# The second half of wq issued from ScalarE's DMA queue, beside the first half on the sync queue, both with 32 KiB rows

## The chip, the cores and the metric

The kernel runs on one core of a Trainium2 chip. The metric is the device time of one execution in microseconds (us); several executions are taken of each kernel, in turns with the kernel it is compared with on the same chip. The profile is one execution more, taken by the hardware profiler; its span is 1.8 us shorter than the device time of the same execution (136.8 against 138.62 for the kernel before).

The engines are PE (TensorE, matmuls; PEld is its weight load), DVE (VectorE), ACT (ScalarE), POOL (GpSimd) and SP (SyncE, which here issues loads only). A name with q (SPq, ACTq) is the engine's instruction sequencer issuing a DMA.

## The reference

One decode step of a transformer layer for a batch of 4, one token each. All tensors are bfloat16.

```python
# B, D = 4, 1024; Hq, Hkv, Dh = 32, 4, 128; Sk = 8192; F = 3584
W = min(4096, max(256, Sk // 4))                       # 2048: the last W keys
q = (layernorm(x) @ wq).reshape(B, 1, Hq, Dh)          # wq 1024 x 4096
scores = einsum(q, k_cache[:, :, Sk-W:]) * Dh ** -0.5  # 8 query heads share one kv head
o = einsum(softmax(scores), v_cache[:, :, Sk-W:])
h = x + o @ wo                                         # wo 4096 x 1024
n = layernorm(h)
out = h + (silu(n @ w1) * (n @ w3)) @ w2               # w1, w3 1024 x 3584; w2 3584 x 1024
```

With four tokens, each weight and each cache entry is used by very few products. The kernel must read wq (8.4 MB), the last 2048 keys and values (8.4 MB each), wo (8.4 MB), w1 and w3 (7.3 MB each) and w2 (7.3 MB): 55.6 MB.

## The kernel before

All large loads go through one pool of five SBUF slots of 32 KiB per partition (4 MiB in all 128 partitions), in one fixed order, on the sync queue. Five slots are filled at the start; each further load is called for when a slot's last reader has been written into the program.

```python
stream = ctx.enter_context(tc.tile_pool(name="stream", bufs=5))
SLOT = 16384; RQ = 4                                   # RQ: chunks of 128 rows of wq in one slot
wq_v = A_wq.rearrange("(p i) n -> p (i n)", i=KC)      # 8 chunks, 8 KiB each per partition

def load_rows(src, n, r0, pieces):
    t = stream.tile([P, SLOT], BF16, tag="s")
    i = 0
    for m in pieces:                                   # one DMA for each piece of m chunks
        nc.sync.dma_start(
            out=t[:, i * n : (i + m) * n], in_=src[:, (r0 + i) * n : (r0 + i + m) * n]
        )
        i += m
    return [t[:, k * n : (k + 1) * n] for k in range(i)]

plan = (
    [("wq", load_rows, (wq_v, N_Q, c, [2, 2] if c == 0 else [4])) for c in range(0, KC, RQ)]
    + [("k", load_kv, (A_k_cache, b)) for b in range(0, B, BS)]
    + ...                                              # v, wo, w1, w3, w2
)
# x_sb <- A_x and later four small loads of x go through nc.scalar
load_next(5)                                           # wq, wq, k, k, v
...
for kc in range(KC):                                   # q = layernorm(x) @ wq : 64 matmuls
    wq_t = loaded["wq"][kc]
    ...
            nc.tensor.matmul(q_ps[...], lhsT=xnT[:, kc, :], rhs=wq_t[:, c0 : c0 + 512],
                             start=(kc == 0), stop=(kc == KC - 1))
    if kc % RQ == RQ - 1:
        load_next()
q_sb = act.tile([P, CQ], BF16)                         # q, scaled, then transposed into qz
...
for u, (b, n) in enumerate(units):                     # K stage: 16 units
    ...                                                # 16 transposes of K on PE into PSUM,
                                                       # copied out by DVE and ACT in turn: kT
    if u >= 1:
        emit_scores(u - 1)                             # 4 matmuls of qz with kT
```

After the K stage come softmax, the product with V (OT_ps), wo (y_ps), the second LayerNorm (hnT), w1 (g_ps), w3 (u_ps), w2 (y_ps again) and the output. The order in which each engine finally runs its instructions is decided when the kernel is built, by a scheduler: it need not be the order of the source.

Of the kernel before, what the change touches and what calls it, by code (L numbers as in the profile page):

```python
# [19 lines left out]
def kernel(  # L20
# [13 lines left out]
    nc = tc.nc  # L34
# [7 lines left out]
    KC = D // P  # L42
# [38 lines left out]
    RQ = 4  # L81
    RO = 16
    BS = 2
    wq_v = A_wq.rearrange("(p i) n -> p (i n)", i=KC)
# [2 lines left out]
    w3_v = B_w3.rearrange("(p i) n -> p (i n)", i=KC)  # L87
    w2_v = B_w2.rearrange("(p i) n -> p (i n)", i=IF)

    def load_rows(src, n, r0, pieces):  # L90

        t = stream.tile([P, SLOT], BF16, tag="s")
        i = 0
        for m in pieces:
            nc.sync.dma_start(  # L95
                out=t[:, i * n : (i + m) * n], in_=src[:, (r0 + i) * n : (r0 + i + m) * n]
            )
            i += m
        return [t[:, k * n : (k + 1) * n] for k in range(i)]

    def load_kv(src, b):
# [11 lines left out]

    N_Q, N_F = Hq * Dh, F
    plan = (
        [("wq", load_rows, (wq_v, N_Q, c, [2, 2] if c == 0 else [4])) for c in range(0, KC, RQ)]
        + [("k", load_kv, (A_k_cache, b)) for b in range(0, B, BS)]
        + [("v", load_kv, (A_v_cache, b)) for b in range(0, B, BS)]
        + [("wo", load_rows, (wo_v, D, c, [RO])) for c in range(0, IO, RO)]
        + [("w1", load_rows, (w1_v, N_F, c, [RQ])) for c in range(0, KC, RQ)]  # L120
        + [("w3", load_rows, (w3_v, N_F, c, [RQ])) for c in range(0, KC, RQ)]
        + [("w2", load_rows, (w2_v, D, 0, [16])), ("w2", load_rows, (w2_v, D, 16, [5, 4, 2, 1]))]
# [349 lines left out]
```

## Time and profile before

| | before |
|---|---|
| time, median of 3 runs | 138.68 us (138.57 to 138.72) |
| span of the profile | 136.8 us |
| bytes read | 55.59 MB |
| q matmuls begin (16, 16 and 32 of them) | 8.2, 12.9, 22.6 us |
| last K scores (start of the softmax maximum) | 57.2 us |
| first gate matmuls (w1) | 94.1 us |
| first matmul on the last piece of w2 | 133.1 us |

First, parts 2 and 3 of the page of the kernel before. DMA is the busy share of the 16 DMA engines in tenths, in 40 equal slices (3.4 us each); GB/s is what they moved; q1 is the sync queue, q10 ScalarE's, q8 the fetches of instructions (packets, MB, share of 16 engines).

```profile
DMA  5999999999999999999999999999999999998950
GB/s 156 437 413 512 393 402 436 421 436 436 417 431 421 436 431 431 431 438 474 460 393 412 426 426 449 427 441 411 436 436 441 427 419 433 441 460 361 420 220 5
...
q1 hardware_dynamic: 3168, 55.58, 95.2%
q8 instruction: 8, 0.13, 0.3%
q10 hardware_dynamic: 60, 0.02, 0.1%
```

The DMA engines are full from the second slice to nearly the last. Almost everything is on the sync queue. Part 4, the chain of waits that ended last, by engine and by line:

```profile
DMA 42%; PE 31%; ACT 12%; DVE 8%; issue 3%; SPq 1%; ACTq 0%; DVEq 0%
DMA t<-in_B_w_dram 26%; DMA t<-in_A_wq_dram 15%; PE kt_ps L261 10%; ACT kT L267 5%; PE scores_ps L246 5%; PE OT_ps L324 5%; PE y_ps L351 5%; ACT z L302 3%; PE q_ps L213 3%; DVE rmax L278 2%; ACT Pm L283 2%; SPq L95 1%; DVE pT L292 1%; PE g_ps L400 1%; DVE z L298 1%
```

Read alone, this chain says that PE and ACT share the blame: 43% of the span. The timeline says how to take it. Its columns are start, duration, engine, line, operation, number, and in brackets how long the engine was idle before and what ended the idleness. L213 are the q matmuls (the second and third stretch wait for wq; the first starts at 8.18 behind a mask that DVE finishes), L278 the first instruction after the last K scores, L400 and L430 the gate, up and last down matmuls; the SPq line is the issue of w1's second half:

```profile
8.18 1.88 PE L213 MATMUL q_ps<-t,xnT 128*4 128x512 bf16 x16 [1.20 <-DVE same L203]
...
12.91 1.87 PE L213 MATMUL q_ps<-t,xnT 128*4 128x512 bf16 x16 [2.86 <-DMA t<-in_A_wq_dram]
...
22.61 3.58 PE L213 MATMUL q_ps<-t,xnT 128*4 128x512 bf16 x32 [7.83 <-DMA t<-in_A_wq_dram]
...
57.21 2.29 DVE L278 TENSOR_REDUCE rmax<-scores_ps 128x1 f32<-128x2048 f32 x1 [1.48 <-PE scores_ps L246]
...
75.71 0.33 SPq L95 DMA_DIRECT2D t<-in_B_w_dram  x1
...
94.12 1.70 PE L400 MATMUL g_ps<-t,hnT 128*32 128x448 bf16 x32 [2.27 <-DVE hnT L388]
99.21 3.17 PE L400 MATMUL g_ps<-t,hnT 128*32 128x448 bf16 x32 [3.39 <-DMA t<-in_B_w_dram]
...
107.66 3.17 PE L400 MATMUL u_ps<-t,hnT 128*32 128x448 bf16 x32 [5.28 <-DMA t<-in_B_w_dram]
...
116.11 3.18 PE L400 MATMUL u_ps<-t,hnT 128*32 128x448 bf16 x32 [5.28 <-DMA t<-in_B_w_dram]
...
133.14 0.41 PE L430 MATMUL y_ps<-t,hgT 128*32 128x256 bf16 x4 [0.24 <-DMA t<-in_B_w_dram]
```

Each stage near the end begins when its load lands. The stages in the middle do not wait for loads, but the loads do not wait for them either: the sync queue issues far ahead. The nearest call is w1's second half, issued at 75.7 us when the first V slot comes free; wo's second half and w1's first half are then still queued or under way.

### The profile page before, as it was taken

To read this page: it belongs to the slowest core of one execution; us is meant where nothing else is said; L and a number is where in the kernel's file an instruction comes from. 1 tells how busy PE (TensorE), PEld (TensorE's weight loads), DVE (VectorE), ACT (ScalarE), POOL (GpSimd) and SP (SyncE) were. 2 spreads that over 40 slices of the span, in tenths; PEclk is the share of its full clock that TensorE was granted. 3 is DMA by queue.
4 is the path that set the end of the run, shared out by engine and by line. 5 is a ranking of instruction groups with operands and counts; after the bars stand their busy time and mean duration, and the time that the engine had idled before them with its cause. 6 is when DMAs were issued, how large, how long until landed. Compare 5 with 4: busy or idle time off the path is not lost.

```text
span 136.8 us, 2307 instructions
## 1 busy us (share of the span) xinstructions
PE 70.0 (51%) x1035; PEld 43.7 (32%) x1035; DVE 42.5 (31%) x73; ACT 31.1 (23%) x36; POOL 1.7 (1%) x8
## 2 busy tenths in 40 slices
PE   0152303799898989503275646954090530802940
PEld 0110001296565656200065644732030210301820
DVE  6440000224343434445962003053003980160000
ACT  0400000126473737354765000000005000000001
POOL 5000000000000000000000000000000000000000
PEclk9999999999999999995555555599959555595595
DMA  5999999999999999999999999999999999998950
GB/s 156 437 413 512 393 402 436 421 436 436 417 431 421 436 431 431 431 438 474 460 393 412 426 426 449 427 441 411 436 436 441 427 419 433 441 460 361 420 220 5
DMA packets 3238, 55.75 MB, mean 407 GB/s; under 512 B 376, under 2 KB 408, under 8 KB 668
## 3 DMA queue, kind: packets, MB, share of 16 engines
q1 hardware_dynamic: 3168, 55.58, 95.2%
q8 instruction: 8, 0.13, 0.3%
q10 hardware_dynamic: 60, 0.02, 0.1%
q14 instruction: 2, 0.02, 0.0%
HBM read 55.59 MB, written 0.01 MB: 406 GB/s over the span
## 4 chain that ended last, share of the span: by engine, by line
DMA 42%; PE 31%; ACT 12%; DVE 8%; issue 3%; SPq 1%; ACTq 0%; DVEq 0%
DMA t<-in_B_w_dram 26%; DMA t<-in_A_wq_dram 15%; PE kt_ps L261 10%; ACT kT L267 5%; PE scores_ps L246 5%; PE OT_ps L324 5%; PE y_ps L351 5%; ACT z L302 3%; PE q_ps L213 3%; DVE rmax L278 2%; ACT Pm L283 2%; SPq L95 1%; DVE pT L292 1%; PE g_ps L400 1%; DVE z L298 1%
## 5 line engine op out<-in xcount | busy, mean ns | idle before, releaser
L267 ACT COPY kT<-kt_ps 128x1024 bf16<-128x1024 bf16 x16 | 15.9, 1013 | 13.0 <-PE kt_ps L261 13.0
L261 PE MATMUL kt_ps<-ident,t 128*128 128x128 bf16 x256 | 17.7, 229 | 0.0
L261 PEld LDWEIGHTS <-t 128*128 128x128 bf16 x256 | 15.7, 103 | 4.9 <-issue 4.9
L265 DVE COPY kT<-kt_ps 128x1024 bf16<-128x1024 bf16 x16 | 11.1, 692 | 16.1 <-PE kt_ps L261 16.1
L213 PE MATMUL q_ps<-t,xnT 128*4 128x512 bf16 x64 | 7.3, 623 | 11.9 <-DMA t<-in_A_wq_dram 10.7
L400 PEld LDWEIGHTS <-hnT 128*32 128x32 bf16 x128 | 4.8, 128 | 21.9 <-issue 19.0
L400 PE MATMUL u_ps<-t,hnT 128*32 128x448 bf16 x64 | 6.4, 575 | 10.6 <-DMA t<-in_B_w_dram 10.6
L324 PE MATMUL OT_ps<-z,t 128*128 128x32 bf16 x256 | 7.5, 188 | 7.6 <-ACT z L302 5.0
L246 PE MATMUL scores_ps<-kT,qz 128*32 128x512 bf16 x64 | 9.9, 609 | 2.9 <-ACT kT L267 2.9
L430 PE MATMUL y_ps<-t,hgT 128*32 128x256 bf16 x112 | 5.8, 374 | 8.4 <-DMA t<-in_B_w_dram 8.4
L324 PEld LDWEIGHTS <-t 128*128 128x128 bf16 x256 | 7.4, 105 | 8.3 <-issue 8.3
L400 PE MATMUL g_ps<-t,hnT 128*32 128x448 bf16 x64 | 4.9, 464 | 5.7 <-DMA t<-in_B_w_dram 3.4
L430 PEld LDWEIGHTS <-hgT 128*32 128x32 bf16 x112 | 4.4, 131 | 10.4 <-issue 6.0
L213 PEld LDWEIGHTS <-xnT 128*4 128x4 bf16 x64 | 2.0, 111 | 16.3 <-issue 16.0
L440 ACT CAST res<-y_ps 128x256 bf16<-128x256 f32 x1 | 0.4, 373 | 28.9 <-PE y_ps L430 28.9
L351 PE MATMUL y_ps<-t,o 128*32 128x256 bf16 x128 | 6.1, 382 | 0.8 <-DVE o L340 0.8
L223 DVE TENSOR_SCALAR q_sb<-q_ps 128x512 bf16<-128x512 f32 x1 | 0.7, 692 | 17.7 <-PE q_ps L213 17.7
L302 ACT ACTIVATE z<-pt_ps,mask 128x512 bf16<-128x512 f32 x8 | 5.3, 687 | 3.5 <-DVE z L298 3.5
L294 PE MATMUL pt_ps<-pT,perm 128*128 128x512 bf16 x4 | 2.4, 607 | 6.8 <-DVE pT L292 6.8
L298 DVE TENSOR_SCALAR z<-pt_ps,mask 128x512 bf16<-128x512 f32 x8 | 5.5, 740 | 1.2 <-ACT z L302 0.8
L414 DVE RECIPROCAL eg<-eg 128x896 f32<-128x896 f32 x1 | 5.8, 5752 | 0.0
L351 PEld LDWEIGHTS <-o 128*32 128x32 bf16 x128 | 4.6, 136 | 3.1 <-DVE o L340 1.9
(73 smaller groups left out, 41.0 us busy)
## 6 DMA issues: line engine op xcount, KB each, us to landing
t<-in_B_w_dram SPq DMA_DIRECT2D x4, 3584.0 KB
t<-in_A_k_cache_dram SPq DMA_DIRECT2D x4, 2048.0 KB, 25.5
t<-in_A_v_cache_dram SPq DMA_DIRECT2D x4, 2048.0 KB, 41.6
t<-in_A_wo_dram SPq DMA_DIRECT2D x2, 4096.0 KB, 40.9
t<-in_A_wq_dram SPq DMA_DIRECT2D x2, 2048.0 KB, 9.6
t<-in_A_wq_dram SPq DMA_DIRECT2D x1, 4096.0 KB, 20.9
t<-in_B_w_dram SPq DMA_DIRECT2D x1, 4096.0 KB, 35.9
t<-in_B_w_dram SPq DMA_DIRECT2D x1, 1280.0 KB, 32.9
```

The costliest lines, as they stand in the source:

```text
L213: nc.tensor.matmul(q_ps[QD * g : QD * g + B, hf * 512 : (hf + 1) * 512], lhsT=xnT[:, kc, :], rhs=wq_t[:, c0 : c0 + 512], start=(kc == 0), ...
L246: nc.tensor.matmul(scores_ps[QD * g : QD * (g + 1), n * 512 : (n + 1) * 512], lhsT=qz[:, b, g * QD : (g + 1) * QD], rhs=kT_v[:, g, :, :], ...
L261: nc.tensor.transpose(out=kt_ps[:, jj, :], in_=k_v[:, n * NJ + t * TB + jj, :], identity=ident[:])
L265: nc.vector.tensor_copy(out=kT[:, t * TB : (t + 1) * TB, :], in_=kt_ps[:])
L267: nc.scalar.copy(out=kT[:, t * TB : (t + 1) * TB, :], in_=kt_ps[:])
L298: nc.vector.tensor_scalar(out=z[:, :, g, :], in0=pt_ps[:], scalar1=mask[:, g : g + 1], scalar2=None, op0=ALU.mult)
L302: nc.scalar.mul(out=z[:, :, g, :], in_=pt_ps[:], mul=mask[:, g : g + 1])
L324: nc.tensor.matmul(OT_ps[:, b, :], lhsT=loaded["v"][b][:, j, :], rhs=PTz[j // NJ][:, (j % NJ) * B + b, :, :], start=(j == 0), stop=(j == J ...
L351: nc.tensor.matmul(y_ps[QD * j : QD * (j + 1), :], lhsT=o4[:, i, :, :].rearrange("p b s -> p (b s)"), rhs=loaded["wo"][i][:, j * CG : (j + ...
L400: nc.tensor.matmul(out_ps[QD * j : QD * (j + 1), hf, :HF], lhsT=hnT[:, k, :], rhs=loaded[kind][k][:, c0 : c0 + HF], start=(k == 0), stop=( ...
L414: nc.vector.reciprocal(out=eg[:], in_=eg[:])
L430: nc.tensor.matmul(y2_ps[QD * j : QD * (j + 1), :], lhsT=hgT[:, i, :], rhs=loaded["w2"][i][:, j * CG : (j + 1) * CG], start=False, stop=(i ...
```

## The change

The intent is that the two halves of wq, the first large thing that PE waits for, are issued from two queues and come in side by side, and that both move in rows of 32 KiB per partition, the first half in one load instead of two.

```diff
-    def load_rows(src, n, r0, pieces):
+    def load_rows(src, n, r0, pieces, eng=nc.sync):
...
-            nc.sync.dma_start(
+            eng.dma_start(
...
-        [("wq", load_rows, (wq_v, N_Q, c, [2, 2] if c == 0 else [4])) for c in range(0, KC, RQ)]
+        [("wq", load_rows, (wq_v, N_Q, c, [4], nc.sync if c == 0 else nc.scalar)) for c in range(0, KC, RQ)]
```

## The prediction

> **What bounds it now: DMA bytes.** In the 40-slice view the DMA row reads 9 from the second slice to nearly the last, at 400 to 460 GB/s. In the trace's DMA packets the weights run back to back, 1.7 to 132.8 us: 55.6 MB in 131 us. After the last landing only 4 us remain. The chain of waits says the same of the end (a w load issued at 97.2, landing at 133.1), but fills its middle, 22.6 to 94 us, with PE and ACT work: those stages run close behind the DMA without holding it up. The sync queue always has work: its loads take 35 to 43 us from issue to landing. The tightest refill is w1's second half, issued at 75.7 when v's first slot comes free, while about 12 us of loads are queued (estimate from the landings).
>
> **What the change does.**
> - Moves an issue (0.42 us) from the sync queue to ScalarE's, ahead of the small x loads and LayerNorm there: about 0.4 us later. No cost: q waits for wq far longer.
> - 16 KiB rows for the first half of wq become 32 KiB. A 16 KiB packet takes 611 ns, a 32 KiB one 1213 ns: over 16 engines 16 x 0.611 = 9.78 against 8 x 1.213 = 9.70, gain 0.07 us.
> - Two rings at once. The Trainium skill, "DMA: Bandwidth & Descriptors", section "Issuing engines are not separate DMA queues", says that loads from both queues run on the same 16 engines and interleave, saving only issue time. The trace before cannot show it (ScalarE's queue carries 0.02 MB), but one ring already moves 433 GB/s with all engines busy: a second has nothing to add.
> - The order of landing changes. Before, wq landed in pieces at 8.1, 12.9 and 22.6 us, and half the q matmuls (2 x 1.88 us) ran under the load. If the rings share evenly, both halves land near 22 to 23, and all matmuls (2 x 3.6 us) come after: q done near 29 instead of 26.2.
> - The built order of PE puts 19 K transposes among and before the q transposes, which hides their 0.7 us wait. K stage ends near 59.4 instead of 57.2 (estimate).
>
> **Critical path.** That 2 us delay runs through softmax, PV and wo, to the first gate matmuls near 96 instead of 94.1. The second gate half waits for w1's landing at 99.2, where PE now idles 3.4 us; the wait shrinks to about 1.3. At 107.7 another 5.3 us of idle follow. So the delay is swallowed, and buffer releases 2 us later eat into a 12 us queue without emptying it. Net -0.07 us, with a small loss possible from interleaving.
>
> **Predicted time: 138.7 us, range 138.1 to 139.5.** Chances: faster by over 2% 0.02, within 2% 0.95, slower by over 2% 0.03.
>
> **What would show the steps right.** DMA row full throughout, 4.2 MB on ScalarE's queue; both wq loads landing within 1.5 us of each other near 22; PE idle from about 8 to 22; K scores ending 1.5 to 3 us later; the wait for w1 before the second gate half shortened by as much; from 99 us on both profiles alike; last landing within 0.7 us of 132.8.
>
> **What would make it wrong.** Two interleaved rings moving less (3% over 20 us is 0.6 us); ScalarE's small loads behind wq holding up its LayerNorm until wq drained (q 8 us later, which could empty the queue); PE's granted clock, 0.5 in parts after 68 us, falling earlier, so that the delay exceeds the 8.7 us of slack; uneven shares, so that the second half finishes late.

## More of the kernel before

One more line will be needed, the score matmuls among the groups of instructions (number, busy us, mean ns, idle before and its cause):

```profile
L246 PE MATMUL scores_ps<-kT,qz 128*32 128x512 bf16 x64 | 9.9, 609 | 2.9 <-ACT kT L267 2.9
```

## The result, and the profile after

| | before | after |
|---|---|---|
| time, median of 4 runs | 138.70 us (138.57 to 138.75) | 138.71 us (138.56 to 138.94) |
| ratio | | 1.0005 (95% interval 0.999 to 1.0019) |
| bytes read | 55.59 MB | 55.59 MB |
| q matmuls begin, q copied out from | 8.2, 26.2 us | 20.0, 26.3 us |
| start of the softmax maximum | 57.2 us | 54.2 us |
| first gate matmuls | 94.1 us | 90.7 us |
| first matmul on the last piece of w2 | 133.1 us | 133.1 us |

Ratios here and below are the mean time of one kernel's runs over that of the kernel before's of the same rounds, so not quite the ratio of the medians quoted. The lines of the page after that answer to those of the page before:

```profile
DMA  5999899999999999999999999999999999998950
GB/s 156 460 460 460 383 388 451 404 450 422 422 450 412 431 441 412 438 441 474 450 412 388 431 432 444 441 428 419 411 470 432 428 411 432 450 460 358 417 226 5
...
q1 hardware_dynamic: 2880, 51.38, 88.0%
q10 hardware_dynamic: 204, 4.22, 7.2%
q8 instruction: 8, 0.13, 0.3%
```

```profile
DMA 80%; PE 16%; SPq 1%; issue 0%; ACT 0%
DMA t<-in_B_w_dram 56%; DMA t<-in_A_k_cache_dram 23%; PE kt_ps L261 9%; PE scores_ps L246 5%; PE g_ps L400 2%; DMA x_sb<-in_A_x_dram 1%; SPq L95 1%; ACT res L440 0%; PE y_ps L430 0%
```

The DMA row is as full as it was; 4.22 MB have moved to ScalarE's queue. The chain of waits now names DMA for 80% of the span, though the time is the same to 0.1%. That is not a new bottleneck. Where stages run close to one another, the chain follows whichever released the next one last, and a shift of 3 us in the middle makes it jump to the other side.

The timeline after, with ACT's issue of the second half as its first line, and the group of the score matmuls:

```profile
1.35 0.39 ACTq L95 DMA_DIRECT2D t<-in_A_wq_dram  x1
...
20.05 6.21 PE L213 MATMUL q_ps<-t,xnT 128*4 128x512 bf16 x64 [12.64 <-DMA t<-in_A_wq_dram]
...
54.17 2.29 DVE L278 TENSOR_REDUCE rmax<-scores_ps 128x1 f32<-128x2048 f32 x1 [1.48 <-PE scores_ps L246]
...
72.67 0.33 SPq L95 DMA_DIRECT2D t<-in_B_w_dram  x1
...
90.70 2.96 PE L400 MATMUL g_ps<-t,hnT 128*32 128x448 bf16 x32 [3.47 <-DMA t<-in_B_w_dram]
99.16 3.18 PE L400 MATMUL g_ps<-t,hnT 128*32 128x448 bf16 x32 [5.50 <-DMA t<-in_B_w_dram]
107.61 3.03 PE L400 MATMUL u_ps<-t,hnT 128*32 128x448 bf16 x32 [5.28 <-DMA t<-in_B_w_dram]
116.07 3.17 PE L400 MATMUL u_ps<-t,hnT 128*32 128x448 bf16 x32 [5.43 <-DMA t<-in_B_w_dram]
...
133.09 0.29 PE L430 MATMUL y_ps<-t,hgT 128*32 128x256 bf16 x4 [0.19 <-DMA t<-in_B_w_dram]
```

```profile
L246 PE MATMUL scores_ps<-kT,qz 128*32 128x512 bf16 x64 | 9.9, 609 | 0.7 <-ACT kT L267 0.7
```

Three things happened. PE did nothing for q until 20.0 us and then all 64 matmuls in 6.2 us, so q was done at the same moment as before. The K stage then took 3 us less: its maximum starts at 54.2 instead of 57.2. And those 3 us ended in a wait: the first gate matmuls, which before came late for a landed w1 (released by hnT), now wait 3.5 us for it. From 99 us on the two profiles are the same to 0.1 us.

The packet records of the trace show the two rings. They bear no engine's number; the line below joins packets of which one starts as the other ends, and so follows one DMA engine. S is the sync queue, A ScalarE's, the number the KiB of a packet, behind @ its start in us.

```
S32@1.7 S32@3.4 S32@4.7 A32@5.9 S32@7.1 A32@8.3 S32@9.5 A32@10.7 S32@11.9 A32@13.1 S32@14.3 A32@15.5 S32@16.8 A32@18.0 A32@19.2 S16@20.4 A32@21.0
```

After the first, each packet of 32 KiB takes 1.21 us whichever ring it comes from, one after another without gaps, and from 4.7 us on the engine takes turns. The first-half load is complete in the records at 18.5 us, but its 4-byte semaphore writes stand at 19.2 to 19.7, after one more packet of the other ring, and PE starts at 20.05. ScalarE's ring was first served at 5.9 us, though its load was issued at 1.35; why the sync queue's ring got three packets ahead of it stays open. Added up, the packets of both kernels had moved the same bytes, to 0.02 MB (0.05 us), at each of 16 moments compared between 5 and 130 us: the second ring neither gained nor lost rate.

### The profile page after: what moved, and what is told of

It is laid out like the page before. It is cut to its first block, busy times and chain, and to the rows that moved or that the text cites. A ratio compares the mean times of both kernels' runs of the same rounds, so it can differ in the third digit from the quotient of the medians.

```text
span 136.8 us, 2306 instructions
## 1 busy us (share of the span) xinstructions
PE 67.5 (49%) x1035; PEld 41.8 (31%) x1035; DVE 42.3 (31%) x73; ACT 31.2 (23%) x36; POOL 1.7 (1%) x8
## 3 DMA queue, kind: packets, MB, share of 16 engines
q10 hardware_dynamic: 204, 4.22, 7.2%
HBM read 55.59 MB, written 0.01 MB: 406 GB/s over the span
## 4 chain that ended last, share of the span: by engine, by line
DMA 80%; PE 16%; SPq 1%; issue 0%; ACT 0%
DMA t<-in_B_w_dram 56%; DMA t<-in_A_k_cache_dram 23%; PE kt_ps L261 9%; PE scores_ps L246 5%; PE g_ps L400 2%; DMA x_sb<-in_A_x_dram 1%; SPq L95 1%; ACT res L440 0%; PE y_ps L430 0%
## 5 line engine op out<-in xcount | busy, mean ns | idle before, releaser
L261 PE MATMUL kt_ps<-ident,t 128*128 128x128 bf16 x256 | 17.5, 220 | 1.5 <-DMA t<-in_A_k_cache_dram 1.5
L261 PEld LDWEIGHTS <-t 128*128 128x128 bf16 x256 | 14.5, 98 | 8.5 <-issue 6.2
L400 PEld LDWEIGHTS <-hnT 128*32 128x32 bf16 x128 | 5.3, 138 | 26.0 <-issue 23.6
L213 PE MATMUL q_ps<-t,xnT 128*4 128x512 bf16 x64 | 6.1, 548 | 12.8 <-DMA t<-in_A_wq_dram 12.6
L400 PE MATMUL g_ps<-t,hnT 128*32 128x448 bf16 x64 | 6.1, 559 | 9.0 <-DMA t<-in_B_w_dram 9.0
L324 PEld LDWEIGHTS <-t 128*128 128x128 bf16 x256 | 7.4, 104 | 7.8 <-issue 7.7
L351 PE MATMUL y_ps<-t,o 128*32 128x256 bf16 x128 | 5.1, 337 | 0.8 <-DVE o L340 0.8
L224 ACT ACTIVATE q_sb<-q_ps 128x512 bf16<-128x512 f32 x1 | 0.6, 597 | 21.1 <-DVE q_sb L223 21.1
```

What stands on the lines that cost most here:

```text
L213: nc.tensor.matmul(q_ps[QD * g : QD * g + B, hf * 512 : (hf + 1) * 512], lhsT=xnT[:, kc, :], rhs=wq_t[:, c0 : c0 + 512], start=(kc == 0), ...
L261: nc.tensor.transpose(out=kt_ps[:, jj, :], in_=k_v[:, n * NJ + t * TB + jj, :], identity=ident[:])
L324: nc.tensor.matmul(OT_ps[:, b, :], lhsT=loaded["v"][b][:, j, :], rhs=PTz[j // NJ][:, (j % NJ) * B + b, :, :], start=(j == 0), stop=(j == J ...
L351: nc.tensor.matmul(y_ps[QD * j : QD * (j + 1), :], lhsT=o4[:, i, :, :].rearrange("p b s -> p (b s)"), rhs=loaded["wo"][i][:, j * CG : (j + ...
L400: nc.tensor.matmul(out_ps[QD * j : QD * (j + 1), hf, :HF], lhsT=hnT[:, k, :], rhs=loaded[kind][k][:, c0 : c0 + HF], start=(k == 0), stop=( ...
```

## The experiments

Eleven kernels were run. The theory: **the number of DMA bytes sets the time, and PE, DVE and ACT have slack.** Its rivals: the compute chain sets the time (the chain of waits before gave it 43% of the span and more); row length or a second ring changes the DMA rate, and the gain or loss was cancelled by something else.

### The two halves of the change, each alone

runs_only: one queue, both halves of wq with 32 KiB rows.

```diff
-[("wq", load_rows, (wq_v, N_Q, c, [2, 2] if c == 0 else [4])) ...]
+[("wq", load_rows, (wq_v, N_Q, c, [4])) ...]
```

> Half of the change: one sync queue, both wq halves as one load of 32 KiB rows each. Theory (the number of DMA bytes sets the time): 138.6 to 138.8 us, ratio to before 0.999 to 1.001; the first half lands near 11.5 to 12.5, the second near 22.6; all q matmuls of the first half under the load, q done near 26.3. The build leaves the order on PE as before, so K scores end near 57.2 us, as before. Rival (row length matters): faster by more than 0.3 us.

Measured: 138.65 us, ratio 1.0000 (0.9987 to 1.0013), five rounds. q was copied out from 26.0 us and the maximum began at 56.9, as before. The first half's last packet ended at 12.4, within the expected 11.5 to 12.5, and its matmuls began at 12.85. Row length alone does nothing that can be seen.

queue_only: the second half on ScalarE's queue, the first still in two loads of 16 KiB rows.

```diff
-[... [2, 2] if c == 0 else [4])) ...]
+[... [2, 2] if c == 0 else [4], nc.sync if c == 0 else nc.scalar)) ...]
```

> Other half of the change: the second half of wq on ScalarE's queue, the first still in two loads of 16 KiB rows on sync. Theory: ratio to before 0.999 to 1.001. The packets of both rings alternate one for one, 16 KiB against 32 KiB, so the second half (ScalarE's) lands first, near 20 to 21.5, and the first half's second piece last, near 21.5 to 23; q done near 26 to 27. The built order on PE is the changed kernel's, so K scores end near 54 us, 3 us before those of the kernel before; if the end of K follows the wq landing and not the order, it stays near 57. Rival (two rings lose or gain rate): ratio outside 0.998 to 1.002.

Measured: 138.68 us, ratio 1.0010 (0.9993 to 1.0026), five rounds. Timeline of PE for q, and of DVE for the maximum:

```profile
12.78 1.88 PE L213 MATMUL q_ps<-t,xnT 128*4 128x512 bf16 x16 [5.39 <-DMA t<-in_A_wq_dram]
22.72 4.15 PE L213 MATMUL q_ps<-t,xnT 128*4 128x512 bf16 x48 [8.06 <-DMA t<-in_A_wq_dram]
...
54.50 2.29 DVE L278 TENSOR_REDUCE rmax<-scores_ps 128x1 f32<-128x2048 f32 x1 [1.48 <-PE scores_ps L246]
```

In the packet records ScalarE's half ends at 19.1 us; the sync queue's second piece is waited for until 22.7. So the half that was issued second was complete first: the rings alternate packet by packet, and the sync ring's packets are half as large. Neither half of the change alone shows an effect on the time beyond the noise, and neither do both together.

### What wq's bytes are worth

half_wq (a wrong result): the second half of wq is never loaded; its matmuls read the first half again. The first half comes in one load on the sync queue.

```diff
-... for c in range(0, KC, RQ)]
+... for c in range(0, RQ, RQ)]
-        wq_t = loaded["wq"][kc]
+        wq_t = loaded["wq"][kc % RQ]
-        if kc % RQ == RQ - 1:
+        if kc == KC - 1:
             load_next()
```

> Wrong result on purpose: the second half of wq is not loaded, its matmuls read the first half again; 4.19 MB less. Theory (bytes set the time): 4.19 MB at 433 GB/s is 9.7 us, so 129.0 us (128.6 to 129.6), ratio 0.930. Rival (the chain of PE and ScalarE work from q to wo sets the time, and the DMA merely keeps up): less than half of it, over 134 us.

Measured: 128.87 us, ratio 0.9295 (0.9283 to 0.9308). 9.8 us less for 4.19 MB is 429 GB/s. All of the missing bytes' time came off, none of it was lost again. The timeline's first gate matmuls still come late, released by hnT; the second, and all stages after them, wait for their loads as before:

```profile
84.54 3.17 PE L400 MATMUL g_ps<-t,hnT 128*32 128x448 bf16 x32 [2.28 <-DVE hnT L388]
89.58 3.18 PE L400 MATMUL g_ps<-t,hnT 128*32 128x448 bf16 x32 [1.86 <-DMA t<-in_B_w_dram]
...
123.67 0.35 PE L430 MATMUL y_ps<-t,hgT 128*32 128x256 bf16 x4 [0.21 <-DMA t<-in_B_w_dram]
```

Taking bytes away makes everything earlier, compute too, so this run alone doesn't refute the compute chain as the limit. The next ones do.

### More compute, the same bytes

delay_7, delay_14 and delay_22: the changed kernel, with the q matmuls done two, three and four times (the first product restarts the accumulation each time, so the result is the same). The loads' order and the order on PE are otherwise those of the changed kernel.

```diff
-    for kc in range(KC):
+    for rep, kc in [(r, k) for r in range(2) for k in range(KC)]:   # 3, 4
...
-        if kc % RQ == RQ - 1:
+        if rep == 1 and kc % RQ == RQ - 1:                          # 2, 3
             load_next()
```

> The changed kernel with the 64 q matmuls done twice (same result, same loads, same order otherwise): 7.2 us of PE work put in between q and K. Theory (bytes set the time, PE has slack): unchanged, ratio 0.999 to 1.002; hnT ready 7 us later, near 94.4, the first gate half starting then instead of at 90.7, and everything from 107.6 us on as before. Rival (the compute chain sets the time): 145.9 us.

> The q matmuls done three times: 14.4 us more PE work between q and K. Theory: the first gate matmuls start near 101.6, the gate and up stage then runs without waits until it has caught up with the landing of the last w3 half near 116. The load of w1's second half, issued at 72.7 in the changed kernel, goes out near 87, 3.6 us before the queue would run dry at 90.7. So still unchanged or up to 1 us longer, 138.6 to 139.7 us. Rival (compute chain): 153 us.

> The q matmuls done four times: 21.6 us more. Theory: now w1's second half is issued near 94.3, after the queue ran dry at 90.7 and with some 2 us from issue to full rate: 4 to 7 us of gap in the DMA row, and the time rises by as much, to 143 to 146 us. Rival (compute chain): 160 us. Rival (more slack than I think): below 141.

| | q copied out from | maximum from | first gate | w1's second half issued | time | ratio to the kernel before (95%) |
|---|---|---|---|---|---|---|
| after | 26.3 | 54.2 | 90.7 | 72.7 | 138.71 | |
| delay_7 | 29.8 | 56.2 | 91.8 | 74.7 | 138.68 | 1.0007 (0.9992 to 1.0022) |
| delay_14 | 33.7 | 60.1 | 96.2 | 78.6 | 140.10 | 1.0106 (1.0091 to 1.0121) |
| delay_22 | 36.4 | 62.8 | 98.3 | 81.3 | 139.95 | 1.0096 (1.0081 to 1.0111) |

Two of the expectations were off. First, the doses were smaller than meant: I had costed a pass at 7.2 us from stretches of 16 and 32 matmuls, but in a long row 64 of them take about 3.5 us (the matmuls that follow the first ones take 0.38 us instead of 0.63 in the records). The delays that reached the softmax were 2.0, 5.9 and 8.6 us. Second, the two longer ones each cost 1.3 us, the larger delay no more than the smaller. A delay on the critical path would not do that. Up to 128 us both are level with the changed kernel in bytes landed, to 0.2 us; the loss is in the last loads. The number of instruction fetches is 9 in both and 8 in the others. That became a theory to test:

more_instr: the changed kernel, with the eight small transposes of x done 17 times while PE waits for wq.

```diff
-    for kc in range(KC):
+    for kc in [k for _ in range(17) for k in range(KC)]:
         nc.tensor.transpose(out=tp_ps[:, kc, :], in_=xn_v[:, kc, :], identity=ident[:B, :B])
```

> The changed kernel with the eight small transposes of x at the start done 17 times (128 more matmuls, 256 more PE instructions, same result), in time in which PE waits for wq anyway; no load, and no work after 20 us, is changed. It tells why the two longer delay runs were both 1.3 us longer. If that comes from the longer instruction stream (one more 16 KiB instruction fetch, the ninth, falling on a DMA engine that has served one already, so that this engine ends its share of the last loads late): 139.9 to 140.1 us, ratio near 1.010, with 9 fetches in the queue of instructions. If it comes from the delay of the compute chain: 138.7 us.

Measured: 140.05 us, ratio 1.0100 (1.0085 to 1.0115), with the maximum at 55.0, less late than in delay_7, which cost nothing. The queue line of its page, and its last down matmuls:

```profile
q8 instruction: 9, 0.15, 0.4%
```

```profile
133.88 1.02 PE L430 MATMUL y_ps<-t,hgT 128*32 128x256 bf16 x12 [1.50 <-DMA t<-in_B_w_dram]
```

So 256 more PE instructions in idle time, one more fetch, cost 1.4 us, and the longer instruction stream is what the two delay runs paid for. That the ninth fetch lands on a DMA engine which has served one already, and that this engine then ends late with its equal share of the last loads, fits the records (the last packet of the last load ends near 134.0 instead of 132.8 us, over a microsecond after nearly all others). In each of the three runs with nine fetches exactly eight of the last load's 128 packets, one engine's share, end after 133.0 us, one behind the other; with eight fetches, none does in the kernels before and after and in delay_7. But the records bear no engine's number: that this engine is the one with two fetches is inferred.

k_odd: the changed kernel with two of the four K loads on ScalarE's queue too.

```diff
-            nc.sync.dma_start(
+            (nc.scalar if k == 1 and src is A_k_cache else nc.sync).dma_start(
                 out=v, in_=src[b + k, ...])
```

> The changed kernel with the K loads of batches 1 and 3 on ScalarE's queue too: twice the bytes run in two rings. In the build the small x loads on ScalarE's queue now wait for the semaphores of the wq loads and the first K load, and LayerNorm's square root stands behind them. Expected: square root near 27 to 29 us instead of 5.7, q done near 37 to 40 instead of 26.3, K scores ending near 64 to 67. Theory (bytes, with over 14 us of slack): the time is still unchanged, ratio 0.998 to 1.003. Rival (compute chain): 11 us longer. Rival (interleaved rings lose rate): 0.5 us or more longer.

Measured: 138.73 us, ratio 1.0008 (0.9991 to 1.0024). The small x loads on ScalarE did wait for earlier loads' semaphores, and the square root of the first LayerNorm, behind them in the same queue, ran at 32.9 us instead of 5.7:

```profile
20.01 11.53 ACTq L146 DMA_DIRECT2D x_q<-in_A_x_dram  x3
31.57 1.28 ACT L160 ACT_TABLE_LOAD   x1 [31.57 <-DMA t<-in_A_k_cache_dram]
32.86 0.29 ACT L160 ACTIVATE rstd<-mv,eps_t 4x1 f32<-4x1 f32 x1
...
85.96 0.33 SPq L95 DMA_DIRECT2D t<-in_B_w_dram  x1
...
103.97 5.68 PE L400 MATMUL g_ps<-t,hnT 128*32 128x448 bf16 x64 [2.27 <-DVE hnT L388]
109.48 1.68 PE L400 MATMUL u_ps<-t,hnT 128*32 128x448 bf16 x32
116.32 3.13 PE L400 MATMUL u_ps<-t,hnT 128*32 128x448 bf16 x32 [5.16 <-DMA t<-in_B_w_dram]
```

q came 15 us later and the maximum at 67.5 us, 13.3 later than in the changed kernel. The first gate matmuls began at 104.0, the gate and the up stage ran through without waiting, and at 116.3 PE again waited for the load. Thirteen microseconds of compute delay, and the time is the same. It also shows a danger of loads on a compute engine's queue, here without a cost.

dve_delay_15 and dve_delay_30: the changed kernel, with q copied to SBUF and multiplied by one 18 or 40 times before use.

```diff
+    q_w = wide.tile([P, CQ], FP32, tag="w4k")
+    nc.vector.tensor_copy(out=q_w[:], in_=q_ps[:])
+    for _ in range(18):                                             # 40
+        nc.vector.tensor_single_scalar(out=q_w[:], in_=q_w[:], scalar=1.0, op=ALU.mult)
-    nc.vector.tensor_single_scalar(out=q_sb[:, :512], in_=q_ps[:, :512], scalar=qscale, op=ALU.mult)
+    nc.vector.tensor_single_scalar(out=q_sb[:, :512], in_=q_w[:, :512], scalar=qscale, op=ALU.mult)
```

> The changed kernel with q copied to SBUF and multiplied by one 18 times on VectorE before use: some 14 us more between q and the K scores, and only some 20 more instructions; the last scores near 62 us, as in the run with 21.6 us nominal delay. If the 1.3 us of those runs came from the instruction stream: 138.7 us, ratio 0.999 to 1.002. If from the delay: 139.9 us or more.

> The same with 40 multiplications: some 30 us between q and the scores, the last scores near 78 us instead of 54, so that w1's second half is issued near 96.5, after the queue has run dry at 90.7. Theory (bytes set the time until a buffer comes free too late): a gap of 6 to 8 us in the DMA row, time 143.5 to 147.5 us. Rival (compute chain sets the time): 162 us or more; rival (compute never matters here): 138.7.

Measured: 140.45 us, ratio 1.0133 (1.0096 to 1.0169), and 156.14 us, ratio 1.1252 (1.1220 to 1.1285). Both delays were longer than meant, since the multiplications also held up DVE's copies of K: the maximum began at 69.6 and 85.4 us, 15.4 and 31.2 after that of the changed kernel. So dve_delay_15 did not tell what it was for; more_instr and k_odd do. What it does tell is where the slack ends. w1's second half was issued at 88.1 us in the one and at 103.9 in the other (timeline of the sync queue). Below are two stretches of dve_delay_15 (busy time of PE, PEld, DVE, ACT and POOL, granted clock, DMA share, GB/s; a packet's whole time counts where it starts, so the share can pass 1), then the DMA row of dve_delay_30, whose slices are 3.85 us long:

```profile
84.00:88.00 4.00, 2.34 (x89) 2.25 (x85) 0.75 (x1) 2.16 (x3) 0.00 (x0) 0.50 1.05 452
88.00:92.00 4.00, 2.99 (x116) 2.89 (x113) 0.00 (x0) 0.00 (x0) 0.00 (x0) 0.79 0.85 312
```

```profile
DMA  7999999999999999995995992008998999998960
GB/s 249 425 417 408 417 438 432 421 434 434 417 442 427 421 442 434 438 476 200 408 408 207 372 394 119 0 4 313 399 458 380 469 391 439 422 476 367 430 237 4
```

In dve_delay_15 the issue at 88.1 came as the queue ran out: the DMA share fell to 0.85 for 4 us, and from then on the landings are 0.6 to 1.1 us behind those of the changed kernel. In dve_delay_30 no load moved from 94.4 to 104.9 us, around the issue at 103.9, and there were two gaps of some 2 us before, near 71 and 84; landings ended some 17 us behind, and the time rose by 17.5. So a delay of 13.3 us behind the changed kernel costs nothing, one of 15.4 costs some 1 us in landings (in time 1.4 in the profiled execution and 1.8 in the median of four), and beyond that each microsecond costs about one. Expectation and measurement differ for dve_delay_30 (143.5 to 147.5 expected, 156.1 measured): the dose was 31 us at the softmax instead of 24, which accounts for some 7 of the 9 to 13 us; the two earlier gaps were not expected either. The rule that a delay costs time only when the queue runs dry held.

### What shortened the K stage

perm: the kernel before with its loads untouched; the q matmuls take the chunks 4 to 7 first, 0 to 3 last.

```diff
+    order = list(range(RQ, KC)) + list(range(RQ))
-    for kc in range(KC):
+    for kc in order:
...
-                    start=(kc == 0),
-                    stop=(kc == KC - 1),
+                    start=(kc == order[0]),
+                    stop=(kc == order[-1]),
```

> The kernel before with nothing changed in its loads; the q matmuls take the chunks 4 to 7 first and 0 to 3 last, so that none can run before 22.6 us. q done near 29.9 instead of 26.3. The built order on PE becomes like the changed kernel's for the first two thirds of the K stage. Theory: time unchanged, ratio 0.999 to 1.001. If the order on PE is what shortened the K stage in the changed kernel, then q done to last scores takes 28 to 29.5 us here instead of 31, with no ScalarE queue at all, ending near 58.5; if the wq landing did it, 31 us, ending near 61.

Measured: 138.67 us, ratio 1.0004 (0.9988 to 1.0019). Timeline of perm (its lines stand one further down in the source):

```profile
22.60 6.34 PE L214 MATMUL q_ps<-t,xnT 128*4 128x512 bf16 x64 [15.53 <-DMA t<-in_A_wq_dram]
...
50.25 0.62 PE L247 MATMUL scores_ps<-kT,qz 128*32 128x512 bf16 x4 [0.60 <-ACT kT L268]
...
57.27 0.62 PE L247 MATMUL scores_ps<-kT,qz 128*32 128x512 bf16 x4 [0.59 <-ACT kT L268]
57.94 2.29 DVE L279 TENSOR_REDUCE rmax<-scores_ps 128x1 f32<-128x2048 f32 x1 [1.48 <-PE scores_ps L247]
```

Its score group:

```profile
L247 PE MATMUL scores_ps<-kT,qz 128*32 128x512 bf16 x64 | 10.5, 609 | 2.6 <-ACT kT L268 2.6
```

| | order on PE in the K stage, as built | q copied out | maximum | between |
|---|---|---|---|---|
| before | of each four units, the fourth's scores stand right behind its own copies | 26.2 | 57.2 | 31.0 |
| runs_only | as before | 26.0 | 56.9 | 30.9 |
| queue_only | scores stand at least one unit behind, to nearly the end | 26.9 | 54.5 | 27.6 |
| after | as queue_only | 26.3 | 54.2 | 27.9 |
| perm | mostly as after at first, as before for the last units | 29.0 | 57.9 | 28.9 |

perm has no large load on ScalarE, and its landings are those of the kernel before, yet it takes 2 us less from q to the maximum. That is the number its expectation asked for, but not the saving of the changed kernel. Nearly all of it lies at the head: in perm the first transposes of K run while q is being copied, in the kernel before 1.8 us after the copy began. From its first transpose of K to the maximum perm takes 29.1 us, the kernel before 29.2, the changed kernel 26.7. In the score groups, the idleness that ACT's copies ended is 2.9 us before, 2.6 in perm and 0.7 after; the fall from 2.9 to 0.7 is 2.2 of the changed kernel's 3 us, and perm has almost none of it.

What ties these waits to the order is seen inside perm. In its units with the order of the changed kernel, scores follow one another every 1.55 us without a wait (37.0 to 41.6 us), as in the changed kernel. In its last four, which have the order of the kernel before, PE waits for ACT where scores stand right behind their own unit's copies (the lines at 50.25 and 57.27), and the four take 7.02 us, against 7.03 in the kernel before. All on one queue, and no load ends any of these waits. But only kernels with the second queue got the changed kernel's order throughout (queue_only, delay_7, delay_14 and delay_22 have it to the instruction, q matmuls left out), so no run shows the whole 3 us with the loads untouched. How the build chooses the order was not looked into.

## Why the prediction was right

The time was predicted at 138.7 us and measured at 138.71, well within 138.1 to 139.5, and the outcome "within 2%" was given 0.95. The mechanism that carried it was right; several of the steps inside the slack were not.

- **"DMA bytes" bound the kernel: right, and shown.** Half of wq taken away took 9.8 us away (half_wq, 9.7 expected). Compute delays of up to 13.3 us at the softmax changed nothing (delay_7, k_odd), and a delay costs time only from where the sync queue runs dry (dve_delay_15, dve_delay_30).
- **"A second has nothing to add": right.** The Trainium skill, "DMA: Bandwidth & Descriptors", section "Issuing engines are not separate DMA queues", says that issuing from several engines only saves issue time. The trace after agrees: packets of both rings take 1.21 us each, in turn, with no gap. The same page's "Queues, rings and completion order" says that an engine goes round the queues packet by packet; the line of packets shows just that from 4.7 us on, though not before, when the sync ring was served three times in a row. What was moved by any moment is the same in both kernels to 0.05 us.
- **"Gain 0.07 us" from 32 KiB rows: too small to be shown.** runs_only gives 1.0000 with an interval of 0.13% on either side, 0.18 us.
- **"Both halves land near 22 to 23, q done near 29": wrong.** The second half did (its last packet ended at 22.7), but the first was used from 20.05 us, since the sync ring had three packets' lead, and the q matmuls in one row took 6.2 us instead of the 7.2 in the sum. q was copied out from 26.3, not 29.
- **"K stage ends near 59.4": wrong, and with the wrong sign.** I took the new order on PE to hide a 0.7 us wait; the K stage ended 3 us earlier in the changed kernel and in queue_only, which has the same order, and some 2.2 us of that are waits for ACT's copies that are gone. The order was there to be read before the prediction: it had changed throughout the stage, and I had costed only its head.
- **"The wait shrinks to about 1.3": wrong.** The wait before the second gate half grew from 3.4 to 5.5 us and a new one of 3.5 appeared before the first, because compute was earlier, not later. The point that mattered, that a shift of the middle either way is swallowed by the wait for w1, held.
- **"A 12 us queue": right in size.** From the changed kernel, 13.3 us of delay were free and 15.4 were not. From the kernel before, whose compute ran 3 us later, that leaves 10 to 12 us (an estimate: the same bounds less 3).

## What to carry to other kernels

When the DMA row is full from end to end, add up the bytes first: no order, queue or engine for a load changes their sum, and a gain anywhere in the middle ends as a longer wait for a load. Don't take a chain of waits as a verdict where stages run close to one another: here its DMA share went from 42% to 80% with no change in time; add a known delay, or take bytes away, and see what moves. And when a change to loads makes the build reorder another engine, compare the whole order, since that may move a stage by more than the loads do.

## What the Trainium skill lacked or had wrong

- "DMA: Bandwidth & Descriptors", section "Bandwidth": it says that for loads from HBM the HBM side, about 358 GB/s, binds rather than the fabric's 435. Here, with the program on one core, the 32 KiB packets of all 16 engines make 16 x 32768 bytes / 1.213 us = 432 GB/s, and half_wq gives 429: the fabric's figure is the one that fits. (The same section does say that its table, which reaches 425 GB/s at 16 MB, is for one core with the other idle, and that 358 is about each core's share when both stream.)
- "DMA: Bandwidth & Descriptors", section "Queues, rings and completion order": no time is given there for what a second busy ring adds to a load's completion. With two rings busy, the first half's last packet ended at 18.5 us, its semaphore writes came at 19.2 to 19.7 after a 1.21 us packet of the other ring, and PE started at 20.05; with one ring before, the last packet ended at 22.25 and PE started at 22.61.
- "Runtime: NRT & Kernel Launch", section "Instruction fetch mechanics": it says that instructions are fetched in 16 KiB blocks of 256, and that the cost of crossing a block's end is "mostly hidden". The first agrees: 256 more PE instructions took the fetches from 8 to 9 (0.15 MB instead of 0.13). The second did not hold in this kernel, whose DMA engines are full: the time was 140.05 us against 138.69 for the kernel before in the same rounds, with no other work or load added after 20 us.
- "DMA: Bandwidth & Descriptors" does not say that a ring served from a later issue can wait: ScalarE's load, issued 0.6 us after the sync queue's, was first served 4 us later, after three 32 KiB packets of the other ring.
